# Attention and feed-forward kernel on one core: chunks 0 and 1 with reciprocals folded and transposed, trimmed scores, another split of the weight conversion, another planner

## The chip, the cores and the metric

The kernel runs on one core of a Trainium2 chip. The time is the device time of one execution in microseconds (us). The median of three runs of the kernel before is 704.7 us (704.69 to 704.81).

## What is computed

Sliding-window attention with sink columns, then a feed-forward layer with a leaky unit. There are 4 batches, 8 heads, 768 positions and a head dimension of 64; the feed-forward layer takes 512 columns to 2048 and back. Inputs are float32 but for the feed-forward weights, which are float64.

```python
scores = scale * np.matmul(q, k.transpose(0, 1, 3, 2))
keep = is_sink | in_window          # pos < 4, or 0 <= row - column < 128
scores = np.where(keep, scores, -1000000000.0)
scores = scores - np.max(scores, axis=-1, keepdims=True)
a = np.exp(scores)
a = a / (np.sum(a, axis=-1, keepdims=True) + 1e-09)
x = np.matmul(a, v)                 # heads side by side: [3072, 512]
h = x @ w_in
g = np.maximum(h, 0.0) + alpha * np.minimum(h, 0.0)
return (g @ w_out).astype(np.float32)
```

## The kernel before

The 3072 rows are cut into 12 chunks of 256 rows (c; three to a batch). A chunk's attention comes first and its feed-forward part behind it. The 2048 inner columns are cut into 16 blocks (f).

**Feed-forward.** Operands are split into a high and a low part of reduced precision, so each product is three matmuls. A first block (`gemm1`, L740, 12 matmuls of 256 columns) takes xh and xl with the weights' two parts. ScalarE then does one activation (L744), VectorE a maximum (L745), ScalarE casts the high part gh (L746), VectorE subtracts for gl (L747). The second block (`gemm2`, L777 and L778 with gh, L775 with gl, 6 matmuls of 512 columns) adds into two banks that stay open over a chunk; it runs two blocks behind its first (LAG).

**Weights.** The 16 weight blocks arrive as pairs of 32-bit words, 1 MB each, and are converted once, by f, in `convert_weights`: ScalarE takes the high words without sign and with a new exponent (L337); VectorE shifts left by three (L340), ors the sign in (L341), ors in the three bits from the low words (L343); ScalarE casts the high part (L348); VectorE subtracts for the low part (L351).

**Attention of chunks 0 and 1** (`SPLIT`). Scores are plain float32 matmuls of 260 columns on two heads at a time in row tiles (L528), then masked row minimum on VectorE (L550) and exponential on ScalarE (L554). `finish_head` transposes each head's unnormalised weights (L573, L574) and copies them out (comb, L578 on ScalarE or L579). `sink_step` makes the reciprocals of the row sums (L611, L613) and the transposed sink weights (L617, L618, L623, L625). `av` for each pair of heads then spreads the reciprocals over a bank with small matmuls against the identity (`ones`, L666), copies them to rb (L669, ScalarE), adds sinks (L670) and values (L680) in the bank's other half, multiplies by rb (L687, VectorE), and splits the product into xh (L691, ScalarE) and xl (L694, VectorE).

**Attention of chunks 2 to 11.** Scores are two reduced-precision matmuls of 260 columns (L537, L538) for each head and half (u) of the chunk. The weights are normalised by head (L583, L584, L591, L595), transposed (`trans`, L637), multiplied by a triangle mask (L641) and used in `av` (chunk 2) or `av_two` (chunks 3 on, L705, L720). In the first half of a batch's first chunk, `soften` reads the last 132 of the 260 score columns only (`w0`).

**What sets the order.** The program first records every operation with a cost, an engine and the values it reads and writes. `Plan.issue` then draws from this record: it holds a clock for each engine, takes for each the operation that can start first (ties by rank, which is the place of the TensorE operation that needs it), and writes the instructions in that order. The order of each engine is thereby fixed before the run. What is recorded in which order is the table `order` at L902 and following: LEAD = 5 blocks of chunk 0, then chunk 1's blocks in turn with chunk 0's rest, so that each weight is used by chunk 1 LEAD blocks after chunk 0; then chunks 2 to 11. `work` puts chunk 1's attention over the first LEAD blocks, chunk 2's over the LATE = 14 blocks ahead of its own, and every later one over the chunk before (SPAN = 12). `convert(f + 2)` keeps the weights two blocks ahead of their first use. `vs_prep` makes the high and low part of the sink values (L410 on ScalarE, L411 on POOL). The startup loads are listed at L425 and following, in the order of their DMAs.

## Time and profile before

| | |
|---|---|
| median of three runs | 704.7 us |
| profiled execution | 704.98 us |
| its span (first to last instruction) | 703.3 us |
| TensorE matmul busy | 686.4 us, 98% |
| VectorE busy | 496.2 us, 71% |
| ScalarE busy | 397.6 us, 57% |
| POOL busy | 33.8 us, 5% |
| granted TensorE clock, mean | 0.994 of full |
| DMA, mean over the span | 91 GB/s |

In the views, PE is TensorE's matmuls, PEld its weight loads, DVE VectorE, ACT ScalarE, POOL GpSimd. An instruction is named by its line in the kernel and by what it writes and reads, as out<-in. A bracket at a row's end is the time for which the engine stood idle before it, and whose work ended that wait. An engine's busy time is no measure of what it costs: which wait ended last is read stage by stage.

### The profile page before, as it was taken

The page shows a single profiled execution, that of the slowest core. Times are in us where ns is not written, and L with a number is a line of the kernel's source. Part 1 is how long each engine was busy: PE and PEld are TensorE (multiplying, and loading weights), DVE is VectorE, ACT ScalarE, POOL GpSimd, SP SyncE. Part 2 cuts the span into 40 slices and gives each one's busy share as a digit, 9 for nine tenths or more (in the row PEclk, how much of TensorE's full clock was granted, in tenths as well). Part 3 has the DMA queues.
Part 4 walks back from the last instruction along what each step waited for, and adds up shares of the span by engine and source line. Part 5 has one row for each costly group of instructions (what it writes and reads, how often), then busy time and mean ns, then how long its engine had stood idle before and what let it go on. Part 6 is the DMA issues. An engine that isn't in the chain of part 4 may idle for free.

```text
span 703.3 us, 13425 instructions
## 1 busy us (share of the span) xinstructions
PE 686.4 (98%) x4737; PEld 600.1 (85%) x4739; DVE 496.2 (71%) x1665; ACT 397.6 (57%) x1090; POOL 33.8 (5%) x116
## 2 busy tenths in 40 slices
PE   7999999989999999999999999999999999999996
PEld 3577898978989989989989988988988988998985
DVE  6699999987746956965964973974974884884331
ACT  5797667856626726735835734843843852753332
POOL 3000000001000000000000000000000000000000
PEclk9899999999999999999999999999999999999999
DMA  8548810443212312321412321420420321300000
GB/s 317 198 142 293 300 65 20 124 126 100 57 47 79 104 46 84 96 59 56 115 43 71 96 61 47 136 62 23 126 76 27 108 76 46 102 6 23 31 2 34
DMA packets 28156, 63.71 MB, mean 91 GB/s; under 512 B 2992, under 2 KB 9136, under 8 KB 28080
## 3 DMA queue, kind: packets, MB, share of 16 engines
q1 hardware_dynamic: 24528, 49.66, 23.3%
q10 hardware_dynamic: 3552, 13.11, 5.2%
q8 instruction: 39, 0.64, 0.4%
q14 instruction: 37, 0.30, 0.1%
HBM read 56.47 MB, written 6.29 MB: 89 GB/s over the span
## 4 chain that ended last, share of the span: by engine, by line
PE 85%; DVE 10%; ACT 2%; issue 2%; DMA 0%; POOL 0%; ACTq 0%; DVEq 0%
PE bank L740 34%; PE bank L775 11%; PE bank L777 11%; PE bank L778 11%; PE bank L720 4%; PE bank L537 3%; PE bank L538 3%; PE bank L637 2%; DVE wa L343 2%; DVE wa L341 2%; DVE w L351 1%; DVE wa L340 1%; PE bank L680 1%; DVE g L745 1%; PE bank L528 1%
## 5 line engine op out<-in xcount | busy, mean ns | idle before, releaser
L740 PE MATMUL bank<-xh,w 128*128 128x256 f32 x1536 | 309.0, 282 | 2.4 <-DVE g L745 2.4
L740 PEld LDWEIGHTS bank<-xh,w 128*128 128x128 f32 x1536 | 250.8, 188 | 9.8 <-DVE g L745 3.3
L740 PE MATMUL bank<-xl,w 128*128 128x256 f32 x768 | 214.3, 279 | 0.5 <-DVE xl L694 0.5
L744 ACT ACTIVATE g<-bank,param 128x256 f32<-128x256 f32 x192 | 89.7, 469 | 140.0 <-PE bank L740 136.4
L777 PE MATMUL bank<-w,gh 128*128 128x512 f32 x382 | 152.4, 399 | 0.0
L778 PE MATMUL bank<-w,gh 128*128 128x512 f32 x382 | 149.7, 392 | 0.0
L740 PEld LDWEIGHTS bank<-xl,w 128*128 128x128 f32 x768 | 144.6, 188 | 5.4 <-DVE xl L694 0.7
L745 DVE TENSOR_TENSOR g<-bank,g 128x256 f32<-128x256 f32 x192 | 80.5, 420 | 87.1 <-ACT g L744 86.7
L775 PE MATMUL bank<-w,gl 128*128 128x512 f32 x382 | 120.4, 397 | 0.0
L746 ACT CAST gh<-g 128x256 fp32r<-128x256 f32 x192 | 77.2, 403 | 74.2 <-DVE g L745 73.4
L554 ACT ACTIVATE pt<-pt,nm 128x260 f32<-128x260 f32 (+1 forms) x192 | 94.5, 493 | 38.5 <-DVE nm L550 35.9
L747 DVE TENSOR_TENSOR gl<-g,gh 128x256 fp32r<-128x256 f32 x192 | 80.9, 422 | 41.1 <-ACT gh L746 38.9
L550 DVE CUSTOM_DVE_ANT_0 pt<-bank,masks 128x260 f32<-128x260 f32 (+1 forms) x192 | 75.9, 400 | 16.2 <-PE bank L538 10.9
L775 PEld LDWEIGHTS bank<-w,gl 128*128 128x128 f32 x382 | 70.0, 188 | 16.2 <-issue 1.7
L777 PEld LDWEIGHTS bank<-w,gh 128*128 128x128 f32 x382 | 71.8, 188 | 8.5 <-ACT comb L578 0.3
L778 PEld LDWEIGHTS bank<-w,gh 128*128 128x128 f32 x382 | 71.8, 188 | 8.2
L641 DVE TENSOR_TENSOR wa<-bank,tri 128x512 f32<-128x512 f32 x80 | 50.6, 684 | 15.2 <-PE bank L637 15.2
L506 DVE TENSOR_TENSOR kq<-stage,kq 64x392 fp32r<-64x392 f32 x80 | 45.2, 565 | 7.6 <-ACT kq L504 5.4
L537 PE MATMUL bank<-kq 128*128 128x260 f32 x160 | 45.0, 285 | 0.5 <-DVE nm L550 0.5
L595 DVE CUSTOM_DVE_ANT_0 comb<-pt,ri 128x128 f32<-128x128 f32 x136 | 44.5, 346 | 0.7
L599 POOL TENSOR_TENSOR sink<-pt,ri 128x8 f32<-128x8 f32 x80 | 20.1, 254 | 513.9 <-DVE ri L584 213.3
L538 PE MATMUL bank<-kq 128*128 128x260 f32 x160 | 44.6, 282 | 0.0
(119 smaller groups left out, 693.5 us busy)
## 6 DMA issues: line engine op xcount, KB each, us to landing
stage<-qk SPq DMA_DIRECT2D x80, 324.0 KB, 2.8
wraw<-w ACTq DMA_DIRECT2D x12, 1024.0 KB, 5.2
v<-vp SPq DMA_DIRECT2D x44, 192.0 KB, 2.5
out_dram<-ob SPq DMA_DIRECT2D x22, 256.0 KB, 2.2
wraw<-w SPq DMA_DIRECT2D x4, 1024.0 KB, 11.1
lent<-pairs SPq DMA_DIRECT2D x4, 324.0 KB, 6.1
stage<-pairs SPq DMA_DIRECT2D x4, 324.0 KB, 6.6
ob<-vs SPq DMA_DIRECT2D x4, 256.0 KB, 3.1
```

The costliest lines, as they stand in the source:

```text
L537: nc.tensor.matmul(s[:, :WIN], qh()[:, qs], ks()[:, ko:ko + WIN], start=True, stop=False)
L538: nc.tensor.matmul(s[:, :WIN], ql()[:, qs], ks()[:, ko:ko + WIN], start=False, stop=True)
L550: op("DVE", dve(n), lambda: nc.vector.tensor_tensor_reduce(out=pt.at[:, u, w0], in0=s.at[:, w0], in1=masks[:, i, w0], scale=-0.125, scalar ...
L554: op("ACT", exp(n), lambda: nc.scalar.activation(pt.at[:, u, w0], pt.at[:, u, w0], AF.Exp, bias=nm.at[:, h, u:u + 1], scale=-1.0, accum_ou ...
L740: nc.tensor.matmul(h(), fin.at[:, 0, part, ks], rhs.at[:, kt], start=(kt == 0 and n == 0), stop=(kt == KT - 1 and n == 2))
L744: op("ACT", act(QC, True), lambda: nc.scalar.activation(g.at, h(), AF.Copy, scale=alt[:, f:f + 1]), reads=[bk, known("param")], writes=[g])
L745: op("DVE", dve(QC), lambda: nc.vector.tensor_tensor(g.at, h(), g.at, ALU.max), reads=[bk], writes=[g])
L746: op("ACT", cast(QC), lambda: nc.scalar.copy(gh.at, g.at), reads=[g], writes=[gh])
L747: op("DVE", dve(QC), lambda: nc.vector.tensor_tensor(gl.at, g.at, gh.at.bitcast(F32), ALU.subtract), reads=[g, gh], writes=[gl])
L775: nc.tensor.matmul(o2[j].at, gl.at[:, js], fin.at[:, 1, 0], start=False, stop=(f == NF - 1))
L777: nc.tensor.matmul(o2[j].at, gh.at[:, js], fin.at[:, 1, 0], start=(f == 0), stop=False)
L778: nc.tensor.matmul(o2[j].at, gh.at[:, js], fin.at[:, 1, 1], start=False, stop=False)
```

## The change

Five parts.

1. Chunks 0 and 1: `av` gives way to `av_split` on two pairs of heads. ScalarE (or VectorE) folds the reciprocals out to a 512-wide tile (L669 of the changed kernel), TensorE transposes it in four pieces into one bank (L745), ScalarE copies the bank (L748), sinks and values of both pairs go into one bank (L754, L711), and one 512-wide multiply (L762), one cast (L766) and one subtraction (L770) end it. Two rb tiles of 256 become one of 512.
2. Scores that nobody reads are left out: in the first half of each batch's first chunk, 132 columns in place of 260.
3. Weight blocks 8 to 15 (LATER): ScalarE writes the three low bits (L386), and one VectorE instruction shifts and ors (L389); the instruction L340 of before falls away for these. Blocks 0 to 7 keep their instructions, the low bits ahead of the sign.
4. The low part of batch 0's sink values is made on VectorE (L460) and no longer on POOL; the loads at the start come in another order.
5. The planner: an engine takes the operation of lowest rank among those that can start within 0.2 us (TensorE 0.1 us) of the first that can; costs of split scores and of changes of tiling are other; LEAD is 7; chunk 1's attention is recorded over the first OVER = 4 blocks.

```diff
@@
 SLACK = 0.5
+WAIT = {"DVE": 0.2, "ACT": 0.2, "PE": 0.1}
...
-LEAD = 5
+LEAD = 7
+OVER = 4
 LATE = 14
 SPAN = 12
 AHEAD = 4
+LATER = 8
...
+                    if pick and t > pick + WAIT.get(e, 0.0):
+                        continue
...
+                    found.append((t, rank[o], i, o, e, real))
+                    if pick is None or t < pick:
+                        pick = t
+                if found:
+                    w = pick + WAIT.get(e, 0.0)
+                    mine = min((x for x in found if x[0] <= w), key=lambda x: x[1:3])
+                    if best is None or mine[:2] < best[:2]:
...
-                    cost += 0.16
+                    cost += 0.16 if "col" in (o.mode, mode) else 0.1
...
-        op("DVE", dve(n, True), lambda: nc.vector.tensor_scalar(wa.at, wa.at, 3, None, op0=ALU.logical_shift_left), writes=[wa])
+        if f < LATER:
+            op("DVE", dve(n, True), lambda: nc.vector.tensor_scalar(wa.at, wa.at, 3, None, op0=ALU.logical_shift_left), writes=[wa])
+            op("DVE", dve(n), lambda: nc.vector.scalar_tensor_tensor(
+                wa.at, low(), 29, wa.at, op0=ALU.logical_shift_right, op1=ALU.bitwise_or), reads=[raw], writes=[wa])
+        else:
+            three = held(None)
+            op("ACT", act(n), lambda: nc.scalar.activation(
+                low(), raw.at.bitcast(U16).rearrange("p x (w s) -> p x w s", s=2)[:, :, 0, 1], AF.Copy, scale=2.0 ** -13, bias=-0.5 + 2.0 ** -14),
+                reads=[raw], writes=[three])
+            op("DVE", dve(n), lambda: nc.vector.scalar_tensor_tensor(
+                wa.at, wa.at, 3, low(), op0=ALU.logical_shift_left, op1=ALU.bitwise_or), reads=[raw, three], writes=[wa])
         op("DVE", dve(n), lambda: nc.vector.scalar_tensor_tensor(
         op("DVE", dve(n), lambda: nc.vector.scalar_tensor_tensor(
             wa.at, high(), -0x80000000, wa.at, op0=ALU.bitwise_and, op1=ALU.bitwise_or), reads=[raw], writes=[wa])
-        op("DVE", dve(n), lambda: nc.vector.scalar_tensor_tensor(
-            wa.at, low(), 29, wa.at, op0=ALU.logical_shift_right, op1=ALU.bitwise_or), reads=[raw], writes=[wa])
...
-        op("POOL", pool2(DM), lambda: nc.gpsimd.tensor_tensor(t.at[D:], raw.at[D:], t.at[D:].bitcast(F32), ALU.subtract), reads=[raw], writes=[t])
+        engine, on, cost = ("POOL", nc.gpsimd, pool2(DM)) if b else ("DVE", nc.vector, dve(DM))
+        op(engine, cost, lambda: on.tensor_tensor(t.at[D:], raw.at[D:], t.at[D:].bitcast(F32), ALU.subtract), reads=[raw], writes=[t])
...
+    then(lambda: load_head(0, 4))
     then(lambda: load_weights(0, "SP"))
     then(lambda: vs_prep(0))
+    then(lambda: load_head(0, 6))
     then(lambda: load_v(0, 0))
-    then(lambda: load_head(0, 4))
-    then(lambda: load_head(0, 6))
     then(lambda: load_v(0, 2))
...
+        w0 = slice(0 if c % CPB or u else P, WIN)
+        n = w0.stop - w0.start
+        kw = slice(ko + w0.start, ko + WIN)
...
-                    nc.tensor.matmul(bk.at[:, :WIN], st.at[r, :QC][:, qs], st.at[r, QC:][:, ko:ko + WIN], start=True, stop=True)
-            op("PE", native(WIN) + 0.02, scores, reads=used, writes=banks_, tail=N_TAIL)
+                    nc.tensor.matmul(bk.at[:, w0], st.at[r, :QC][:, qs], st.at[r, QC:][:, kw], start=True, stop=True)
+            op("PE", 1.47 * native(n), scores, reads=used, writes=banks_, tail=N_TAIL, mode="row")
...
-                nc.tensor.matmul(s[:, :WIN], qh()[:, qs], ks()[:, ko:ko + WIN], start=True, stop=False)
-                nc.tensor.matmul(s[:, :WIN], ql()[:, qs], ks()[:, ko:ko + WIN], start=False, stop=True)
-            op("PE", 2 * mm(WIN), scores, reads=[kq], writes=banks_, tail=R_TAIL)
+                nc.tensor.matmul(s[:, w0], qh()[:, qs], ks()[:, kw], start=True, stop=False)
+                nc.tensor.matmul(s[:, w0], ql()[:, qs], ks()[:, kw], start=False, stop=True)
+            op("PE", 2 * mm(n), scores, reads=[kq], writes=banks_, tail=R_TAIL)
...
-            r = rinv[c, g] = val("ri")
+            r, wide = val("ri"), val("ob")
+            rinv[c, g] = wide
...
+            op("DVE", 0.16, lambda: nc.vector.reciprocal(four(), four()), writes=[r])
+            each = lambda: r.at.rearrange("p (h u) -> p u h", u=2).unsqueeze(3).broadcast_to([P, 2, 4, D])
+            fold = lambda: wide.at.rearrange("p (u h d) -> p u h d", u=2, h=4)
+            op("ACT", cast(8 * D), lambda: nc.scalar.copy(fold(), each()), reads=[r], writes=[wide],
+               other=("DVE", dve(8 * D, True), lambda: nc.vector.tensor_copy(fold(), each())))
...
-            def ones():
-                for u in range(2):
-                    for j in range(2):
-                        x = 2 * (p % 2) + j
-                        nc.tensor.matmul(r()[j * D:(j + 1) * D, u * P:(u + 1) * P],
-                                         rv.at[:, 2 * x + u:2 * x + u + 1].broadcast_to([P, D]), ident, start=True, stop=True)
-            op("PE", native(P), ones, reads=[rv, known("ident")], writes=[(bk, 1)], tail=N_TAIL, mode="col")
...
+    def av_split(c, g):
+        both = (2 * g, 2 * g + 1)
+        src, v = [wt.pop((c, x)) for x in both], [vtile.pop((c, x)) for x in both]
+        wide, rb = rinv[c, g], val("rb")
+        rk = val("o" if c == 0 else "pa")
+
+        def inverse():
+            for n in range(2):
+                for u in range(2):
+                    nc.tensor.transpose(rk.at[:, (2 * n + u) * P:(2 * n + u + 1) * P],
+                                        wide.at[:, (2 * u + n) * P:(2 * u + n + 1) * P], ident)
+        op("PE", 4 * TURN, inverse, reads=[wide, known("ident")], writes=[rk], tail=T_TAIL)
+        op("ACT", cast(4 * P, True), lambda: nc.scalar.copy(rb.at, rk.at), reads=[rk], writes=[rb])
+        bk = val("pa")
+        vt, st = vst[c // CPB], sinkT[c]
+
+        def sinks():
+            for n, x in enumerate(both):
+                nc.tensor.matmul(bk.at[:, n * QC:(n + 1) * QC], vt.at[:, x * P:(x + 1) * P], st.at, start=n == 0, stop=False)
+        op("PE", 2 * mm(QC), sinks, reads=[vt, st], writes=[bk], tail=R_TAIL)
+
+        def both_values():
+            for n in range(2):
+                values(c, v[n].at, lambda j: src[n][j].at, bk.at[:, n * QC:(n + 1) * QC], n == 1)
+        op("PE", 2 * values_cost(c), both_values, reads=[t for two in src for t in two] + v, writes=[bk], tail=N_TAIL, mode="col")
+        x1, x2 = begin_x(c, 2 * g)
+        op("DVE", dve(4 * P), lambda: nc.vector.tensor_tensor(rb.at, bk.at, rb.at, ALU.mult), reads=[bk], writes=[rb])
+        view = lambda: rb.at.rearrange("p (n x) -> p n x", n=2)
+        part = slice(2 * g, 2 * g + 2)
+        keys = [(x1, x) for x in both], [(x2, x) for x in both]
+        op("ACT", cast(4 * P), lambda: nc.scalar.copy(x1.at[:, part], view()), reads=[rb], writes=keys[0])
+        if c and not g:
+            for x in both:
+                load_v(c, x + 2)
+        op("DVE", dve(4 * P), lambda: nc.vector.tensor_tensor(x2.at[:, part], view(), x1.at[:, part].bitcast(F32), ALU.subtract),
+           reads=[rb, *keys[0]], writes=keys[1])
...
-    several("rb", 2, [P, QC], F32)
+    several("rb", 1, [P, 2 * QC], F32)
...
-            for at, st in ((8, lambda: av(c, 3)), (8, lambda: av(c, 2)), (8, lambda: sk(1)),
-                           (6, lambda: av(c, 1)), (5, lambda: av(c, 0)), (4, sk)):
+            for at, st in ((8, lambda: av_split(c, 1)), (8, lambda: sk(1)), (5, lambda: av_split(c, 0)), (4, sk)):
...
-    work = spread(attention(1), LEAD)
+    work = spread(attention(1), OVER) + [[] for _ in range(LEAD - OVER)]
...
```

`values` holds the value matmuls of `av` as they were, on a bank given to it; `begin_x` opens xh and xl. `link`, `draw` and `issue` are the former `issue` in three functions.

**VectorE, second half of chunk 0's softmax beside the first weight block.** wa_85 is the first weight's working tile, ri_93 the first four heads' reciprocals, ts_100 their sink weights, pt_79 and pt_80 the masked scores of two heads. Before:

```order
L340 TENSOR_SCALAR wa_85<-wa_85 128x1024
L341 SCALAR_TENSOR_TENSOR wa_85<-wraw,wa_85 128x1024
L611 TENSOR_SCALAR ri_93<-sm_91 128x8
L343 SCALAR_TENSOR_TENSOR wa_85<-wraw,wa_85 128x1024
L617 CAST ts_100<-sink_87 128x4x32
L613 RECIPROCAL ri_93<-ri_93 128x8
L550 ISA pt_79,nm_89<-bank_64,masks 128x132
L550 ISA nm_89 128x1
L618 TENSOR_TENSOR ts_100<-sink_87,ts_100 128x4x32
L550 ISA pt_80,nm_89<-bank_65,masks 128x132
```

In the changed kernel:

```order
L381 TENSOR_SCALAR wa_85<-wa_85 128x1024
L460 TENSOR_TENSOR vs_102<-ob_103,vs_102 64x512
L664 TENSOR_SCALAR ri_93<-sm_91 128x8
L674 CAST ts_100<-sink_87 128x4x32
L675 TENSOR_TENSOR ts_100<-sink_87,ts_100 128x4x32
L666 RECIPROCAL ri_93<-ri_93 128x8
L602 ISA pt_79,nm_89<-bank_64,masks 128x132
L602 ISA nm_89 128x1
L602 ISA pt_80,nm_89<-bank_65,masks 128x132
L602 ISA nm_89 128x1
L382 SCALAR_TENSOR_TENSOR wa_85<-wraw,wa_85 128x1024
L391 SCALAR_TENSOR_TENSOR wa_85<-wraw,wa_85 128x1024
```

The low part of the sink values (L460) has come in, the sink weights and the two softmax rows (L550, now L602) stand ahead of both or instructions of the weight, and in before they stood behind both.

**TensorE, middle of chunk 2's attention.** comb_82 and comb_83 are normalised weights of two pairs of heads, sinkT_101 and vs_102 the sinks, wa_85 and v_76 weights and values, bank_65 takes chunk 3's scores; xh_106 is an input of the feed-forward block. Before:

```order
L637 MATMUL bank_67<-ident,comb_82 128x128 x4
L775 MATMUL bank_66<-w_1226,gl_115 128x512
L775 MATMUL bank_64<-w_1226,gl_115 128x512
L537 MATMUL bank_65<-kq_74 128x260
L538 MATMUL bank_65<-kq_74 128x260
L670 MATMUL bank_66<-sinkT_101,vs_102 128x256
L680 MATMUL bank_66<-wa_85,v_76 64x256 x2
L680 MATMUL bank_66<-wa_85,v_76 64x128 x4
L637 MATMUL bank_67<-ident,comb_83 128x128 x4
L537 MATMUL bank_65<-kq_75 128x260
L538 MATMUL bank_65<-kq_75 128x260
```

In the changed kernel:

```order
L806 MATMUL bank_69<-xh_106,w_1129 128x256
L725 MATMUL bank_66<-sinkT_101,vs_102 128x256
L711 MATMUL bank_66<-wa_85,v_76 64x256 x2
L711 MATMUL bank_66<-wa_85,v_76 64x128 x4
L806 MATMUL bank_69<-xh_106,w_1129 128x256
L806 MATMUL bank_69<-xl_108,w_1129 128x256
L806 MATMUL bank_69<-xh_106,w_1129 128x256 x2
L806 MATMUL bank_69<-xl_108,w_1129 128x256
L806 MATMUL bank_69<-xh_106,w_1129 128x256 x2
L806 MATMUL bank_69<-xl_108,w_1129 128x256
L806 MATMUL bank_69<-xh_106,w_1129 128x256
L843 MATMUL bank_67<-w_1046,gh_113 128x512
```

Before, sinks, values, transposes and scores follow each other with no feed-forward matmul among them; in the changed kernel sinks and values of a pair stand between the matmuls of a first block (L806 is L740 of before).

## Rows read from the trace of the kernel before

**Rows 1.** Busy time by stretch: start:end, length, then PE, PEld, DVE, ACT, POOL, clock.

```profile
28.00:52.00 24.00, 23.47 (x172) 16.08 (x171) 23.72 (x62) 21.45 (x61) 2.62 (x8) 1.00 0.47 148
52.00:73.40 21.40, 19.05 (x151) 14.80 (x150) 20.21 (x39) 16.59 (x38) 1.33 (x2) 1.00 0.85 310
73.40:100.00 26.60, 26.60 (x174) 24.16 (x173) 26.54 (x42) 18.21 (x33) 0.00 (x0) 1.00 0.58 198
73.40:182.10 108.70, 105.08 (x709) 93.32 (x708) 97.15 (x284) 72.91 (x183) 4.79 (x15) 1.00 0.35 109
182.00:703.30 521.30, 515.58 (x3600) 463.51 (x3598) 338.55 (x1217) 270.19 (x763) 19.19 (x69) 1.00 0.22 65
```

**Rows 2.** The chain that ended last, shares of the span by engine.

```profile
PE 85%; DVE 10%; ACT 2%; issue 2%; DMA 0%; POOL 0%; ACTq 0%; DVEq 0%
```

**Rows 3.** Timeline of VectorE, startup: start, duration, engine, line, operation.

```profile
11.80 2.24 DVE L341 SCALAR_TENSOR_TENSOR wa<-wraw,wa 128x1024 int32<-128x1024 int32 x1
...
21.49 0.30 DVE L550 CUSTOM_DVE_ANT_0 pt<-bank,masks 128x132 f32<-128x132 f32 x1 [2.46 <-PE bank L528]
...
23.33 0.42 DVE L687 TENSOR_TENSOR rb<-bank,rb 128x256 f32<-128x256 f32 x1 [1.54 <-ACT rb L669]
...
25.16 0.42 DVE L694 TENSOR_TENSOR xl<-rb,xh 128x256 fp32r<-128x256 f32 x1 [1.20 <-ACT xh L691]
```

**Rows 4.** Timeline of POOL, startup.

```profile
11.69 1.27 POOL L411 TENSOR_TENSOR vs<-ob,vs 64x512 fp32r<-64x512 f32 x1 [3.28 <-ACT vs L410]
```

**Rows 5.** Timeline of TensorE, startup.

```profile
15.77 1.65 PE L528 MATMUL bank<-lent 64*128 64x260 f32 x4 [2.09 <-DVE nm L550]
```

**Rows 6.** Groups by line, whole span: count, busy us, mean ns, idle before.

```profile
L341 DVE SCALAR_TENSOR_TENSOR wa<-wraw,wa 128x1024 int32<-128x1024 int32 x16 | 20.5, 1282 | 0.1
L337 ACT ACTIVATE wa<-wraw 128x1024 f32<-128x1024 f32 x16 | 18.4, 1151 | 3.9 <-DVE w L351 3.8
L340 DVE TENSOR_SCALAR wa<-wa 128x1024 int32<-128x1024 int32 x16 | 10.9, 685 | 0.5 <-ACT wa L337 0.5
L666 PE MATMUL bank<-ident,ri 128*64 128x128 f32 x64 | 5.6, 304 | 0.0
L641 DVE TENSOR_TENSOR wa<-bank,tri 128x512 f32<-128x512 f32 x80 | 50.6, 684 | 15.2 <-PE bank L637 15.2
L506 DVE TENSOR_TENSOR kq<-stage,kq 64x392 fp32r<-64x392 f32 x80 | 45.2, 565 | 7.6 <-ACT kq L504 5.4
```

**Rows 7.** Timeline of VectorE, last subtraction of chunk 1's attention.

```profile
69.41 0.42 DVE L694 TENSOR_TENSOR xl<-rb,xh 128x256 fp32r<-128x256 f32 x1
```

**Rows 8.** Timeline of TensorE, from the last wait ahead of the full stretch.

```profile
71.96 0.38 PE L740 MATMUL bank<-xh,w 128*128 128x256 f32 x1 [1.57 <-DVE g L745]
...
73.42 0.39 PE L777 MATMUL bank<-w,gh 128*128 128x512 f32 x1
...
76.19 0.39 PE L777 MATMUL bank<-w,gh 128*128 128x512 f32 x1
```

**Rows 9.** Timeline of TensorE, chunk 2's attention.

```profile
148.29 0.28 PE L538 MATMUL bank<-kq 128*128 128x260 f32 x1
148.41 0.40 PE L777 MATMUL bank<-w,gh 128*128 128x512 f32 x1
...
154.55 0.39 PE L670 MATMUL bank<-sinkT,vs 128*128 128x256 f32 x1 [1.44 <-DVE wa L641]
154.86 1.09 PE L680 MATMUL bank<-wa,v 128*64 128x256 f32 x12
155.88 0.66 PE L637 MATMUL bank<-ident,comb 128*128 128x128 f32 x4
156.30 0.36 PE L740 MATMUL bank<-xh,w 128*128 128x256 f32 x1
```

**Rows 10.** Groups by line, TensorE, 73.4 to 182.1 us.

```profile
L777 PE MATMUL bank<-w,gh 128*128 128x512 f32 x65 | 25.5, 393 | 0.0
...
L537 PE MATMUL bank<-kq 128*128 128x260 f32 x30 | 8.8, 298 | 0.5 <-DVE nm L550 0.5
```

More of the change, by code (lines that the diff above doesn't have):

```diff
@@ L1 @@
+from bisect import insort
 from collections import deque
@@ new lines, in draw @@
+            clock[e] = t + cost
+            if o.locks and (e == "DVE" or e == "POOL"):
+                lock = t + cost
+            if o.nbytes:
+                dma = max(dma, t + 1.5) + o.nbytes / 290e3
+                end = dma + 0.5
+            else:
+                end = t + cost + o.tail
+            for v in o.values:
+                left[v] -= 1
+                if not left[v] and v.kind:
+                    insort(free[v.kind], (end + self.HOP, at[v]), key=lambda f: f[0])
+            for a in o.after:
+                i = a.index
+                x = t + cost if e == a.engine == "PE" else end + self.HOP
+                ready[i] = max(ready[i], x)
+                sure[i] = max(sure[i], x + (0.0 if e == "PE" else SLACK))
+                missing[i] -= 1
+                if not missing[i]:
+                    for w in a.ways:
+                        open_[w].append(a)
@@ L675, in av @@
         sets.append((2, slice(3 * P, 4 * P), slice(P, 2 * P)))
[L677 to L682 removed]
+        for n, (blk, ws, os) in enumerate(sets):
+            for j in range(2):
+                nc.tensor.matmul(a[j * D:(j + 1) * D, os], v[:, blk, j], weights(j)[:, ws], start=False, stop=stop and n == len(sets) - 1)
```

209 lines of the change are left out of this document (94 added, 115 removed).

## The prediction

> **What bounds the kernel now.** I read the chain of waits first: TensorE holds 85% of it and VectorE 10% [rows 2]. The busy times by stretch say where each counts. From 182 us to the end TensorE is busy for 515.6 of 521.3 us [rows 1], so there only matmul time and TensorE's own waits count. From 28 to 73 us VectorE is busy for 43.9 of 45.4 us: weights, chunk 1's attention and the first blocks share it. From 73.4 to 100 us both are full (26.60 and 26.54 of 26.60), while ScalarE has 8.4 us free [rows 1]. In the timeline, TensorE's last wait of that start is the one of 1.57 us on L745; from 73.42 us it runs without a gap [rows 8] up to chunk 2's attention, where it waits 1.44 us for the mask multiply L641 [rows 9]. So three numbers are wanted: how early the state of 73.42 us is reached, what the waits around 154 us are worth, and how many matmul nanoseconds go.
>
> The profiled execution took 704.98 us, its span 703.3; the sum is made against 704.98, and the median of the runs stands 0.28 below. A measurement of this kernel can tell some 0.2% (1.4 us) from no change: faster is below 703.3, slower above 706.1.
>
> **Startup, to 28 us.** VectorE waits 2.46 us for scores (L528), 1.54 for the copy of the reciprocals (L669), 1.20 for xh (L691), and the sign instruction L341 takes 2.24 us [rows 3] where the other fifteen average 1.22 ((20.5 − 2.24)/15, [rows 6]); POOL's L411 ran beside it from 11.69 for 1.27 us [rows 4]. Together 6.2 us. The change attacks each. L411's work goes to VectorE, where a 64x512 subtraction is bounded by half and all of L641's 0.68 for 512 elements [rows 6]; I take 0.6, plus 0.45 for one comb copy that the new order gives to VectorE (near the 0.42 of a 256-wide pass, [rows 3]). The order rows show the softmax of the last heads ahead of the weight's ors; the 2.09 us that scores waited at 15.77 us for L550 [rows 5], which stood behind those ors, is what made VectorE wait 2.46 us later. The first weight's load stands behind 324 KB more, some 1.1 us at the 310 GB/s of a full stretch [rows 1]; the softmax now placed ahead covers it, and if that cover fails the first weight is 1.1 us late. All gone, it is −6.2 + 1.05 = −5.2; none gained, 0. The folded path is a serial chain of its own (fold, four transposes, copy, values, multiply, cast), so I leave 0.7 of waiting: **−4.5**.
>
> **28 to 73 us.** LEAD = 7 and OVER = 4 put more in front of chunk 1's last xl, which ends at 69.83 us now [rows 7]. Counted along both VectorE orders: one weight's two ors more (2 × 1.22), one block's maximum and subtraction more (2 × 0.42), one head's preparation less (0.57 [rows 6] and 0.43), six multiplies and subtractions of 256 (0.42 each, [rows 3]) against three of 512 (0.68, by L641, the nearest row) −0.5: +1.8, less small ones, +1.6. ScalarE gets 3.2 us more (an L337 of 1.15 [rows 6], a low-bit pass, folds, an activation), against 7.4 us that it has free there [rows 1]; a quarter of it taken as exposed, +0.8 (ends 0 and 3.2). So the last xl ends at 69.8 − 4.5 + 1.6 + 0.8 = 67.7. By then TensorE has done half a first block less and one second block more than at 73.42 us; both halves of a pair count 2.77/2 us (76.19 − 73.42, [rows 8]), so it is 0.7 ahead: 67.0. Behind that xl, weight 7 still needs 2.6 us of VectorE while TensorE has 1.6 us of work: +1.0. For waits on L745 like the 1.57 one I allow another 1.0. 69.0 against 73.42: **−4.4**. The removed `ones` (64 matmuls, 5.6 us busy, two at a time [rows 6]) give way to 16 transposes of 0.105 us (four from 155.88 to 156.30, [rows 9]); half lie in the start, where TensorE waits anyhow, so I count nothing, with −1.2 as the far end.
>
> **73 to 145 us.** VectorE's conversion for f ≥ 8 loses one L340 each, 8 × 0.685 = 5.5 us [rows 6], and ScalarE gains eight low-bit passes. TensorE has no gap here now [rows 1], so a lighter VectorE yields nothing; but LEAD = 7 needs each weight two blocks, 5.5 us, earlier, and the 5.5 us pays for just that. The low-bit pass on ScalarE shows in no row; the nearest is L337, 1.15 us with 1024 elements at the same 8-byte distance. A pair of pairs (5.54 us) leaves ScalarE 8.39/26.6 × 5.54 = 1.75 us free, so 1.15 fits: **0**. Its far end is L341's disturbed 2.24 us: 8 × 0.49 = +3.9.
>
> [...]
>
> **Chunk 2's attention.** From 73.4 to 182.1 us are 108.7 us, 105.1 busy [rows 1]: 3.6 us of plain waiting. By count: L777 runs twice in a second block, and 64 such (the 65th opens the next) are 32 pairs [rows 10], × 2.77 = 88.6; 60 score matmuls (30 and 30) of 0.12 us (148.41 − 148.29) = 7.2; four sets of values of 1.02 (155.88 − 154.86), four of transposes of 0.42, four of sinks of 0.31 = 7.0 [rows 9]. That is 102.8, so up to 5.9 us are lost. The order rows show sinks and values of a pair between feed-forward matmuls in the changed kernel, where before they followed each other and L641. Ends: −5.9 and 0 (or worse, if the waits only move). I take **−3.8**, near the plain waits.
>
> **Trimmed scores.** Chunks 3, 6 and 9: 3 × 8 × 2 = 48 matmuls from 260 to 132 columns, now 0.12 us. By columns 0.061 (−2.8 us); no gain, 0; at the pace of plain float32, 640 columns in the 1.02 us of a value set, 1.6 ns each, 0.21 us (+4.3). The nearest row in size is the transposes' 0.105 for 128 columns: 48 × 0.015 = **−0.6**. Chunk 0's trimmed scores lie in the start and are in its term.
>
> **Steady state.** The TensorE order from about 182 us is all but the same: 0.
>
> Sum: −4.4 − 3.8 − 0.6 = −8.8; 696.2 for a profiled execution, **696.0** as median.
>
> **Rivals.**
> - *The start's gain is lost* (17%): the fold chain replaces the waits by its own, or the weights, needed 5.5 us earlier, come late and TensorE waits for L351 in the leading blocks. For: VectorE is full to 100 us. Against: the 5.5 us taken off it. 696.2 + 4.4 − 0.3 = 700.3.
> - *The hole stays or moves* (10%): L641 and the normalisation are late again. For: VectorE still does it all. 699.7.
> - *Trimmed scores run at the float32 pace* (7%): no row has a reduced-precision matmul under 256 columns. 696.0 + 0.6 + 4.3 = 700.9.
> - *The change does not do what it says* (5%): start and hole both as before. 704.2, within 0.2%.
> - *Slower* (6%): ScalarE becomes the bound of 73 to 122 us. Its low-bit pass reads two bytes in eight, a form that no row has. Each us above the free 1.75 delays eight weights, and behind them the blocks that need them; 8 × (d − 1.75) exceeds 8.8 from d = 2.85 us. At d = 3.5 it is +14.0, so 710. Against: L337's 1.15 at the same distance.
>
> **Numbers.** The forecast has 55%. Its own range is 696.0 with −0.7 (startup), −2.1 (hole), −2.2 (scores) and the allowance of 1.0 as the low end, 690.5 rounded; the four rivals on the high side up to 701 lie inside 702.0. Left out are the last two (11%) and what lies beyond the far ends. Faster 0.55 + 0.17 + 0.10 + 0.07 = 0.89; same 0.05; slower 0.06.
>
> **What would show it.** Right: VectorE's waits of 2.46, 1.54 and 1.20 us gone before 28 us; the first sign instruction at 1.22; chunk 1's last subtraction (L770) ending near 67.7; TensorE without gaps from about 69; waits of at most 2.1 us about chunk 2's attention; trimmed L537-like matmuls 0.105 us apart; the low-bit pass at 1.05 to 1.2 us. Wrong: TensorE waits on L351 or on xl after 70 us, a low-bit pass over 1.75 us, trimmed scores over 0.12 us, or a new wait in the steady stretch.

## The result and the profile after

The changed kernel takes 695.81 us as median of four runs (695.09 to 696.52); the kernel before took 704.70 (704.11 to 704.81) beside it. The ratio is 0.9875 with a 95% interval of 0.9858 to 0.9893, so it is faster by 8.9 us. The profiled execution took 695.24 us, its span 693.3, 10.0 us less than before's. Busy time by stretch in the changed kernel (length, then PE, PEld, DVE, ACT, POOL, granted clock):

```profile
10.00:28.00 18.00, 16.95 (x112) 9.72 (x116) 16.25 (x46) 17.05 (x48) 2.73 (x6) 1.00 0.84 311
28.00:52.00 24.00, 21.48 (x142) 15.90 (x143) 23.35 (x52) 21.91 (x55) 3.16 (x6) 0.93 0.71 249
52.00:69.00 17.00, 16.33 (x116) 13.84 (x115) 16.48 (x30) 15.68 (x33) 0.87 (x2) 1.00 0.49 182
69.00:100.00 31.00, 30.39 (x199) 27.47 (x200) 30.84 (x48) 27.91 (x47) 0.00 (x0) 1.00 0.55 191
100.00:145.00 45.00, 44.89 (x299) 39.96 (x299) 40.98 (x145) 29.54 (x83) 1.62 (x8) 1.00 0.27 82
145.00:166.00 21.00, 20.33 (x150) 17.50 (x151) 14.51 (x53) 13.12 (x39) 2.04 (x4) 1.00 0.32 102
166.00:182.00 16.00, 16.00 (x111) 14.73 (x110) 14.44 (x61) 11.56 (x36) 1.04 (x5) 1.00 0.28 85
182.00:693.30 511.30, 505.51 (x3541) 455.22 (x3539) 335.00 (x1189) 267.53 (x747) 17.85 (x66) 1.00 0.21 65
```

From 69 to 182 us TensorE stands idle for 113.0 − (30.39 + 44.89 + 20.33 + 16.00) = 1.4 us, where before it stood for 3.6 in 73.4 to 182.1 [rows 1]. ScalarE is now nearly as full as VectorE up to 100 us. The clock, which was at 0.83 or less from 15 to 24 us before (first fence), now falls later, from 38 to 42 us (second):

```profile
15.00:18.00 3.00, 1.89 (x5) 1.20 (x7) 2.09 (x13) 1.44 (x3) 0.00 (x0) 0.53 1.02 400
18.00:21.00 3.00, 3.00 (x16) 1.69 (x14) 1.03 (x1) 1.73 (x7) 0.19 (x1) 0.50 1.04 411
21.00:24.00 3.00, 3.00 (x27) 1.82 (x23) 0.94 (x5) 1.10 (x6) 0.19 (x1) 0.83 0.62 229
```

```profile
36.00:39.00 3.00, 1.97 (x10) 1.40 (x10) 2.84 (x11) 2.62 (x7) 0.96 (x2) 0.86 0.79 318
39.00:42.00 3.00, 3.00 (x16) 2.34 (x15) 2.97 (x8) 2.75 (x10) 0.17 (x1) 0.58 0.37 107
```

VectorE's timeline in the changed kernel, for [rows 3, 7]: the three waits are gone, the first sign and or instructions take their 1.22 us, and chunk 1's last subtraction ends at 66.4 us.

```profile
14.49 1.22 DVE L382 SCALAR_TENSOR_TENSOR wa<-wraw,wa 128x1024 int32<-128x1024 int32 x1
15.75 1.23 DVE L391 SCALAR_TENSOR_TENSOR wa<-wraw,wa 128x1024 int32<-128x1024 int32 x1
...
19.29 0.29 DVE L602 CUSTOM_DVE_ANT_0 pt<-bank,masks 128x132 f32<-128x132 f32 x1
...
19.71 0.69 DVE L762 TENSOR_TENSOR rb<-bank,rb 128x512 f32<-128x512 f32 x1
...
22.08 0.68 DVE L770 TENSOR_TENSOR xl<-rb,xh 128x512 fp32r<-128x512 f32 x1
...
65.73 0.68 DVE L770 TENSOR_TENSOR xl<-rb,xh 128x512 fp32r<-128x512 f32 x1
```

**Where the time went.** The order of first blocks differs, but their number at a point of the work does not, so each trace is read at three points: the start of the 17th first block (193rd matmul of L740, now L806), of the 49th (577th), and of the 189th. Before, these are at 96.9, 211.8 and 683.4 us. Between the first two lies chunk 2's attention, between the last two the stretch that repeats. Offsets against before in us, profiled executions, with the medians of the runs:

| kernel | 17th | 49th | 189th | median us |
|---|---|---|---|---|
| changed | −5.9 | −8.8 | −10.1 | 695.8 |
| e1 all columns | −4.7 | −7.6 | −8.5 | 696.9 |
| e2 no window | −6.4 | −6.6 | −7.0 | 697.5 |
| e3 small matmuls | −0.3 | −3.4 | −4.7 | 700.5 |
| e4 low bits on VectorE | −4.9 | −0.6 | −1.9 | 702.7 |
| e5 sinks on POOL | −4.6 | −5.3 | −6.6 | 699.7 |
| e6 LEAD 5 | −4.3 | −5.4 | −6.7 | 698.7 |
| e7 clock held | −5.3 | −8.6 | −9.9 | 695.0 |
| e8 before, clock held | −1.9 | −1.9 | −1.9 | 704.1 |
| e9 before, folded | +4.4 | +2.7 | +2.5 | 707.3 |
| e10 small matmuls, clock held | −2.4 | −5.3 | −6.6 | 698.6 |
| e11 old loads | −5.3 | −6.0 | −7.3 | 698.1 |
| e12 two more on ScalarE | −4.2 | −3.8 | −5.1 | 698.7 |

The medians stand beside runs of the kernel before on the same chip, whose medians were 704.74 (e1 to e4), 704.74 (e5 to e8) and 704.26 (e9 to e12). A row of offsets is one execution. Those of e2 and e12 are the longest of their four runs: 698.36 us against 697.11 to 697.57, and 700.19 against 698.49 to 698.93.

### The profile page after: what moved, and what is told of

Its sections match the earlier page's. It is cut to its first block, busy times and chain, and to the rows that moved or that the text cites. A ratio compares the mean times of both kernels' runs of the same rounds, so it can differ in the third digit from the quotient of the medians.

```text
span 693.3 us, 13330 instructions
## 1 busy us (share of the span) xinstructions
PE 680.6 (98%) x4694; PEld 598.1 (86%) x4696; DVE 497.2 (72%) x1651; ACT 408.2 (59%) x1093; POOL 32.2 (5%) x115
## 4 chain that ended last, share of the span: by engine, by line
PE 86%; DVE 9%; ACT 3%; issue 1%; POOL 0%; DMA 0%; ACTq 0%; DVEq 0%
PE bank L806 35%; PE bank L841 12%; PE bank L843 12%; PE bank L844 11%; PE bank L711 5%; PE bank L589 3%; PE bank L590 3%; PE bank L694 3%; DVE wa L391 2%; DVE w L399 1%; ACT pt L606 1%; DVE wa L389 1%; ACT wa L377 1%; DVE gl L813 1%; DVE g L811 1%
## 5 line engine op out<-in xcount | busy, mean ns | idle before, releaser
L806 PE MATMUL bank<-xh,w 128*128 128x256 f32 x1536 | 314.2, 283 | 1.4 <-DVE g L811 1.2
L806 PEld LDWEIGHTS bank<-xh,w 128*128 128x128 f32 x1536 | 252.7, 189 | 9.2 <-DVE g L811 2.0
L806 PE MATMUL bank<-xl,w 128*128 128x256 f32 x768 | 214.6, 279 | 0.0
L844 PE MATMUL bank<-w,gh 128*128 128x512 f32 x382 | 149.9, 392 | 0.0
L806 PEld LDWEIGHTS bank<-xl,w 128*128 128x128 f32 x768 | 145.1, 189 | 5.2
L811 DVE TENSOR_TENSOR g<-bank,g 128x256 f32<-128x256 f32 x192 | 80.4, 420 | 88.6 <-ACT g L810 87.8
L606 ACT ACTIVATE pt<-pt,nm 128x260 f32<-128x260 f32 (+1 forms) x192 | 94.2, 491 | 24.5 <-DVE nm L602 23.9
L602 DVE CUSTOM_DVE_ANT_0 pt<-bank,masks 128x260 f32<-128x260 f32 (+1 forms) x192 | 75.0, 402 | 15.2 <-PE bank L590 11.9
L844 PEld LDWEIGHTS bank<-w,gh 128*128 128x128 f32 x382 | 71.9, 188 | 8.3
L555 DVE TENSOR_TENSOR kq<-stage,kq 64x392 fp32r<-64x392 f32 x80 | 45.2, 566 | 10.1 <-ACT kq L553 8.1
L553 ACT CAST kq<-stage 128x392 fp32r<-128x392 f32 x80 | 41.5, 519 | 8.9 <-PE bank L590 6.2
L590 PE MATMUL bank<-kq 128*128 128x260 f32 (+1 forms) x160 | 44.3, 281 | 0.0
L589 PE MATMUL bank<-kq 128*128 128x260 f32 (+1 forms) x160 | 43.8, 278 | 0.1
```

Of the source, the lines that this page charges most:

```text
L589: nc.tensor.matmul(s[:, w0], qh()[:, qs], ks()[:, kw], start=True, stop=False)
L590: nc.tensor.matmul(s[:, w0], ql()[:, qs], ks()[:, kw], start=False, stop=True)
L602: op("DVE", dve(n), lambda: nc.vector.tensor_tensor_reduce(out=pt.at[:, u, w0], in0=s.at[:, w0], in1=masks[:, i, w0], scale=-0.125, scalar ...
L606: op("ACT", exp(n), lambda: nc.scalar.activation(pt.at[:, u, w0], pt.at[:, u, w0], AF.Exp, bias=nm.at[:, h, u:u + 1], scale=-1.0, accum_ou ...
L806: nc.tensor.matmul(h(), fin.at[:, 0, part, ks], rhs.at[:, kt], start=(kt == 0 and n == 0), stop=(kt == KT - 1 and n == 2))
L811: op("DVE", dve(QC), lambda: nc.vector.tensor_tensor(g.at, h(), g.at, ALU.max), reads=[bk], writes=[g])
```

## The experiments

**e1, trimming undone.** The matmuls of L580, L589 and L590 take all 260 columns; every engine's order stays.

```diff
...
-                nc.tensor.matmul(s[:, w0], qh()[:, qs], ks()[:, kw], start=True, stop=False)
+                nc.tensor.matmul(s[:, :WIN], qh()[:, qs], ks()[:, ko:ko + WIN], start=True, stop=False)
...
```

> The changed kernel with all 260 score columns again (chunks 0, 3, 6, 9, first half); every engine's order stays. My theory: in the trace of the changed kernel the two trimmed matmuls of a head start 60 and 113 ns apart where untrimmed ones take 119 each, so 24 heads times 65 ns = 1.6 us come back in chunks 3, 6 and 9, and the sixteen float32 matmuls of chunk 0 add up to 1 us in the startup: 697.0 to 698.5 as median. Rival (the forecast's price, 15 ns each): 0.7 us, 696.5. Rival (trimming mattered in the start only): no difference behind 200 us.

696.91 us, ratio to before 0.9899 (0.9877 to 0.9922), 1.1 over the changed kernel, but not where I said. The two intervals overlap (the changed kernel's is 0.9858 to 0.9893), so the pieces are read from the traces. The offset to the changed kernel is 1.2 at the 17th block, 1.2 at the 49th and 1.6 at the 189th: chunk 0's trimmed float32 matmuls are worth some 1.2 us in the start, chunk 3 nothing that can be read, and chunks 6 and 9 some 0.2 us each. Why so little is seen in TensorE's timeline of one head, in the changed kernel and in this one:

```profile
317.00 0.22 PE L589 MATMUL bank<-kq 128*128 128x132 f32 x1
317.06 0.28 PE L590 MATMUL bank<-kq 128*128 128x132 f32 x1
317.17 0.44 PE L843 MATMUL bank<-w,gh 128*128 128x512 f32 x1
317.45 0.40 PE L844 MATMUL bank<-w,gh 128*128 128x512 f32 x1
```

```profile
318.19 0.28 PE L589 MATMUL bank<-kq 128*128 128x260 f32 x1
318.31 0.28 PE L590 MATMUL bank<-kq 128*128 128x260 f32 x1
318.43 0.40 PE L843 MATMUL bank<-w,gh 128*128 128x512 f32 x1
318.66 0.39 PE L844 MATMUL bank<-w,gh 128*128 128x512 f32 x1
```

From the first score matmul to L844 it is 0.45 us trimmed and 0.47 untrimmed: the first of the pair gains 60 ns, and the long matmul behind holds its successor back by 50 (0.28 against 0.23). My expectation took the first gap for the gain; the forecast's 15 ns a matmul was close.

**e2, the planner's window off.** Rank decides only between operations that can start at the same time, as before; costs, LEAD and all else as changed.

```diff
-WAIT = {"DVE": 0.2, "ACT": 0.2, "PE": 0.1}
+WAIT = {}
```

> The changed kernel with the planner's window set to nothing, so that each engine again takes the operation that can start first. My theory: the gaps about chunk 2's attention were closed by the order in which its sinks and values are drawn, so they come back (2.4 to 3.5 us between 140 and 175 us), and the start loses part of its gain: 699 to 701. Rival: LEAD and the lighter VectorE closed them, then the gaps stay closed and the time is within 1 us of 695.8.

697.50 us, 0.9898 (0.9881 to 0.9914). The start did not lose (−6.4 against −5.9). The stretch of chunk 2's attention gains 0.2 us here where the changed kernel gains 2.9, but not because the gaps came back. Between the 17th and the 49th block TensorE stands idle for 3.6 us in the kernel before, 0.8 in the changed kernel and 1.3 here, and the wait of 1.44 us for the mask multiply [rows 9] is missing here too. Of the 2.6 us that this execution takes more than the changed kernel there, 0.5 are idle time and 2.1 longer busy time; the clock is at half from 157 to 161 us:

```profile
157.16 0.40 PE L806 MATMUL bank<-xh,w 128*128 128x256 f32 x1 [0.62 <-DVE g L811]
```

```profile
156.00:159.00 3.00, 2.36 (x12) 2.14 (x12) 2.94 (x13) 2.72 (x11) 0.00 (x0) 0.73 0.48 139
159.00:162.00 3.00, 3.00 (x15) 2.63 (x14) 1.96 (x9) 1.99 (x6) 0.36 (x2) 0.70 0.28 93
```

The three other runs are some 1 us shorter at a mean clock of 0.995 to 0.996 and not 0.993, so they probably lack that fall; they have no trace. So my theory fails for the gaps: they stay mostly closed without the window. The rival is not shown either, since runs below with LEAD = 7 and the window stand idle for 2.8 us in this stretch (e5, e11). From the 49th to the 189th block e2 gains 0.4 where the changed kernel gains 1.3: the window is worth 0.9 us in the stretch that I had called unchanged.

**e3, small matmuls put back.** `av_split` gives way to the former work on one pair, without the fold.

```diff
...
-            for at, st in ((8, lambda: av_split(c, 1)), (8, lambda: sk(1)), (5, lambda: av_split(c, 0)), (4, sk)):
+            for at, st in ((8, lambda: av_ones(c, 3)), (8, lambda: av_ones(c, 2)), (8, lambda: sk(1)),
+                           (6, lambda: av_ones(c, 1)), (5, lambda: av_ones(c, 0)), (4, sk)):
```

> The changed kernel with chunk 0's and 1's values done as before: one pair at a time, reciprocals spread by small matmuls against the identity, multiplies and subtractions 256 wide. My theory: VectorE has six more narrow passes and TensorE eight more rounds of small matmuls in the start, together 1.5 to 3 us at the point where TensorE becomes full, nothing behind it: 697.3 to 698.8. Rival (the folded chain was the cure of the startup waits): all of the 5.9 us of the start come back, 701.7. Rival (that part is hidden): 695.8 within 0.5.

700.53 us, 0.9950 (0.9934 to 0.9966): 4.7 us over the changed kernel, and all of it in the start (−0.3 at the 17th block), beyond my range and near the rival's. Its clock is low for longer (36 to 48 us: 0.95, 0.50, 0.50, 0.91), which e10 takes apart.

**e10, the same with the clock held.** As e3, with the unread matmuls of e7.

> The changed kernel with the small matmuls and narrow passes put back (as in the third run) and with the unread matmuls that keep TensorE busy between 28 and 45 us (as in the seventh). Theory A: most of the 4.7 us lost in the third run is the half clock that its trace shows from 38 to 46 us; held, 2 us or more come back: at most 698.5. Theory B: it is VectorE's narrow passes and the waits on them, and the clock is worth what it was in the seventh run, 0.8 us: 699.4 to 700.2.

698.57 us, 0.9920 (0.9903 to 0.9937), with the clock at 1.00 from 36 to 48 us. 2.0 us come back, between the two theories' numbers at their border: of e3's 4.7 us about 2 are the low clock that its waits bring on, and against e7 (the clock held in both) 3.6 us remain for the narrow passes, the small matmuls and the order that the planner draws with them. (The two ran on different chips, where the kernel before takes 704.74 and 704.26 us.)

**e9, the fold alone in the kernel before.** `av_split`, the fold and the single 512-wide rb, nothing else of the change (its diff is the one of the change for these functions).

> The kernel before with the first part of the change alone: reciprocals folded, transposed and copied 512 wide, values of two pairs in one bank, 512-wide multiply, cast and subtraction; planner, LEAD, loads, weights and score columns as before. My theory (from the run with the small matmuls put back): this part is the larger half of the start's gain, 3 to 5 us; the gaps about chunk 2's attention stay: 699.7 to 701.7. Rival: it gains only in the new planner's order, and here the time is within 1 us of 704.7.

707.27 us, 1.0041 (1.0028 to 1.0053): **slower** by 3.0 us, so a part that is missed by 3.6 us or more when the changed kernel goes without it costs 3 us when the old one takes it in. The timelines of VectorE, ScalarE and TensorE from 67 us show how:

```profile
67.07 1.22 DVE L351 TENSOR_TENSOR w<-wa,w 128x1024 fp32r<-128x1024 f32 x1
68.21 0.69 DVE L740 TENSOR_TENSOR rb<-bank,rb 128x512 f32<-128x512 f32 x1
```

```profile
68.33 1.14 ACT L337 ACTIVATE wa<-wraw 128x1024 f32<-128x1024 f32 x1 [1.34 <-DVE w L351]
69.37 0.20 ACT L337 ACTIVATION_READ_ACCUMULATOR wa<-wraw 128x1 f32 x1
69.47 0.61 ACT L744 CAST xh<-rb 128x512 fp32r<-128x512 f32 x1
```

```profile
70.13 0.38 PE L794 MATMUL bank<-xh,w 128*128 128x256 f32 x1 [3.03 <-ACT xh L744]
...
71.29 0.39 PE L794 MATMUL bank<-xl,w 128*128 128x256 f32 x1 [0.78 <-DVE xl L748]
...
73.89 0.58 PE L794 MATMUL bank<-xh,w 128*128 128x256 f32 x1 [1.75 <-DVE g L799]
```

The wide multiply stands behind weights that were ready a little earlier, the cast of xh behind another weight's first pass; TensorE waits 3.03, 0.78 and 1.75 us for what it needs next, and its clock is at 0.56 and 0.50 in the two stretches from 72 to 78 us. Between the 17th and the 49th block this kernel gains 1.7 us (table), with the old planner and the old LEAD: there, too, a redrawn order moves the time. This is the rival of the prediction in which the folded chain replaces the old waits by its own, and the planner decides whether it comes.

**e4, the low bits on VectorE for all weights.**

```diff
-LATER = 8
+LATER = 16
```

> The changed kernel with all sixteen weights converted as blocks 0 to 7 are, so no low-bit pass on ScalarE. My theory: VectorE is full from 28 to 100 us and has 5.5 us more to do by the last conversion, while LEAD = 7 wants each weight two blocks earlier; TensorE waits for the weights' low part: 2 to 5 us, 698 to 701. Rival: VectorE's work behind 73 us has room (TensorE is the only bound there), 695.8 within 0.5. [...]

702.74 us, 0.9974 (0.9961 to 0.9987): 6.9 us over the changed kernel, more than expected. Only 1.0 of it is in the start. Most of the rest comes at 126 us, and not by a late weight: scores wait for VectorE's L602, which is behind. VectorE's last conversion (L399) starts at 112.5 us here and at 106.5 in the changed kernel.

```profile
126.78 0.39 PE L589 MATMUL bank<-kq 128*128 128x260 f32 x1 [0.42 <-DVE nm L602]
...
127.91 0.36 PE L589 MATMUL bank<-kq 128*128 128x260 f32 x1 [0.62 <-DVE nm L602]
...
129.49 0.39 PE L589 MATMUL bank<-kq 128*128 128x260 f32 x1 [1.11 <-DVE nm L602]
...
130.61 0.56 PE L589 MATMUL bank<-kq 128*128 128x260 f32 x1 [0.62 <-ACT kq L553]
```

```profile
126.00:129.00 3.00, 1.34 (x6) 0.59 (x4) 2.84 (x13) 2.96 (x11) 0.20 (x1) 1.00 0.59 173
129.00:132.00 3.00, 1.89 (x8) 1.72 (x9) 2.85 (x13) 2.55 (x8) 0.20 (x1) 0.65 0.74 192
132.00:135.00 3.00, 3.00 (x14) 2.84 (x13) 1.35 (x8) 1.63 (x5) 0.21 (x1) 0.50 0.78 258
135.00:138.00 3.00, 3.00 (x16) 2.63 (x15) 1.73 (x10) 1.70 (x6) 0.21 (x1) 0.71 0.01 3
```

These waits sum to 2.8 us, and TensorE works on at half clock for nearly 7 us. From the 17th to the 49th block e4 takes 7.2 us more than the changed kernel: 3.5 more of idle TensorE (4.3 against 0.8) and 3.6 more of busy time, near the 3.4 us by which the clocks of the three stretches from 129 us (0.65, 0.50, 0.71) fall short of full, an estimate from the fence. So in this order the low-bit passes on ScalarE are worth most of the change's margin, about half of it by the clock; the planner's order was redrawn with them. A pass over 1024 elements took 0.685 us on VectorE (L340, [rows 6]) and 1.17 on ScalarE (L386 in the changed kernel), a ratio of 1.7, and VectorE was the fuller engine: in e4 it is busy for 2.96 to 3.00 of every 3 us from 96 to 111 us, ScalarE for 1.04 to 2.61. The 1.17 is near the 1.15 taken from L337 [rows 6].

**e12, two more low-bit passes on ScalarE** (LATER = 6, with the clock held as in e7).

> The seventh run's kernel (the clock held) with the low bits of weights 6 and 7 on ScalarE too. My theory: ScalarE is busy for 15.7 of 17 us from 52 to 69 us and 27.9 of 31 from 69 to 100, so two more passes of about 1.2 us find no free time and TensorE waits for gh and for the weights' high part: 0.5 to 2.5 us over 695.0. Rival: VectorE is the tighter of the two there, and 1.4 us less on it gives 0.3 to 1 us: 694.0 to 694.7.

698.74 us, 0.9918 (0.9902 to 0.9935), 3.7 over e7: slower as expected, by more. But in its trace TensorE's longest waits from 60 us on are on L606 (the line that is L602 in the changed kernel: 0.92 us at 74.8, 1.43 at 157.2), and for gh once 0.19. VectorE in turn waits for ScalarE between 28 and 130 us: 1.2 us for the activation (L814) and 0.8 for the low-bit pass (L390), waits that e7 lacks. So ScalarE has a part in it, but its share against that of the new order is not shown. In the profiled execution, the longest of the four, the clock also falls, from 159 to 163 us.

**e5, e6, e11: one other part undone each.** The sinks' low part on POOL; LEAD at 5; the startup loads in their old order.

```diff
-        engine, on, cost = ("POOL", nc.gpsimd, pool2(DM)) if b else ("DVE", nc.vector, dve(DM))
+        engine, on, cost = "POOL", nc.gpsimd, pool2(DM)
```

> The changed kernel with the low part of batch 0's sink values on POOL again, as for the other batches. My theory: POOL's subtraction and VectorE's weight instruction beside it slow each other as before (1.0 us on L341 there), against 0.69 us that VectorE no longer does itself; the start is 0.3 to 1.0 us later: 696.1 to 696.9. Rival (the move was a main part of the start's gain): 2 us or more, over 697.8. Rival (no contention in the new order): 695.1 to 695.5.

```diff
-LEAD = 7
+LEAD = 5
```

> The changed kernel with LEAD at 5 as before (chunk 1's attention still over 4 blocks). My theory: five leading blocks give TensorE less to do while chunk 1's softmax and the weights share VectorE, so it waits for chunk 1's xl and its clock may fall again: 1 to 4 us, 696.8 to 699.8. Rival: the later use of each weight makes up for it, and the time is within 0.5 us of 695.8. The gaps about chunk 2's attention stay closed by both.

```diff
-    then(lambda: load_head(0, 4))
     then(lambda: load_weights(0, "SP"))
     then(lambda: vs_prep(0))
-    then(lambda: load_head(0, 6))
     then(lambda: load_v(0, 0))
+    then(lambda: load_head(0, 4))
+    then(lambda: load_head(0, 6))
     then(lambda: load_v(0, 2))
```

> The changed kernel with the loads at the start in their old order (the first weight ahead of the third and fourth pair of heads). My theory: the first weight comes 1 us earlier and the third pair's scores later; VectorE waits for those scores as before, and the start is 0.5 to 1.5 us later: 696.3 to 697.3. Rival: no difference, 695.8 within 0.4. Rival: earlier weights gain, 694.8 to 695.3.

699.68 (0.9931, 0.9911 to 0.9952), 698.72 (0.9927, 0.9900 to 0.9954) and 698.08 us (0.9908, 0.9892 to 0.9925). In e5 the longer VectorE instruction that I expected is there: the one beside POOL's subtraction takes 2.25 us. It is L382 here, where it was L341 before, and the sign instruction L391 now takes its 1.22. That POOL is slowed in turn is not shown: its subtraction takes 1.27 us here, as in the changed kernel at 152 to 468 us, behind the last conversion (L460, 1.269 to 1.277):

```profile
12.39 1.27 POOL L460 TENSOR_TENSOR vs<-ob,vs 64x512 fp32r<-64x512 f32 x1 [3.67 <-ACT vs L458]
```

```profile
12.50 2.25 DVE L382 SCALAR_TENSOR_TENSOR wa<-wraw,wa 128x1024 int32<-128x1024 int32 x1
```

In e6 the expected wait is there, 2.09 us on L811 at 66.05 us, and the clock falls at its end (0.51 from 66 to 69 us). My prices for e5 and e11 were too low by 2.8 us and by 0.8, and e5's median lies where its rival had it (the move a main part of the start's gain), though the trace does not put it in the start. e5's runs lie in two pairs, 698.7 us at a mean clock of 0.998 and 700.6 to 700.9 at 0.993, and the median stands between them. At the 17th block e5 and e11 stand only 1.3 and 0.6 us behind the changed kernel; the rest is lost about chunk 2's attention, where all three, and e12, show the same wait, which the changed kernel lacks (row of e5, whose matmuls behind it take 0.28 and 0.40 us as ahead of it, at a mean clock of 0.998 for the execution):

```profile
157.27 0.39 PE L589 MATMUL bank<-kq 128*128 128x260 f32 x1 [1.44 <-DVE nm L602]
```

An edit in the first 20 us thus moves the planner's order 130 us later: TensorE's order in the traces of e5 and e11 differs from the changed kernel's there, and is the same again behind the 49th block. Those 2 us belong to the redrawn order and not to POOL or to a load.

**e7, the clock held.** Matmuls of 248 unread columns where the planner sees TensorE idle between 28 and 45 us.

```diff
...
+    def spare():
+        nc.tensor.matmul(banks[5][:, 264:512], idle[:, :1].broadcast_to([P, P]), idle[:, 1:].broadcast_to([P, 248]), start=False, stop=True, skip_group_check=True)
-    plan.issue(steps, fill, WARM)
+    plan.issue(steps, fill, WARM, spare, 45.0)
```

> The changed kernel with 26 matmuls more whose results nobody reads (248 columns each, in the unread half of a bank) where the planner sees TensorE idle between 28 and 45 us. My theory: TensorE's idle 33 to 38 us is what lets its clock fall to half from 38.5 to 41.7 us; held busy, it keeps the full clock, and the 1.6 us of work that the half clock costs come back in part: 694.0 to 695.3, the clock at 1.00 in all stretches. Rival (VectorE bounds this stretch, so the low clock costs nothing): 695.8 within 0.4, at a clock of 1.00. Rival (the idle matmuls stand in front of scores and delay them): 696.5 or more.

694.99 us (694.16 to 695.35), 0.9855 (0.9839 to 0.9872). The clock is at 1.00 from 36 to 45 us. The median is 0.8 us under the changed kernel's, within the expected numbers, but the intervals overlap and its profiled execution is not ahead: VectorE is busy for 8.52 of the 9 us from 36 us on, and the gain is not settled. Its median is the lowest of the study.

**e8, the kernel before with its clock held** by eight unread matmuls of 512 columns ahead of the scores that waited 2.09 us [rows 5].

```diff
...
             def scores():
+                if (c, h, u) == HOLD:
+                    for _ in range(8):
+                        nc.tensor.matmul(banks[5], idle[:, :1].broadcast_to([P, P]), idle[:, 1:].broadcast_to([P, 512]), start=True, stop=True)
```

> The kernel before with eight unread matmuls (512 columns) in the 2.09 us for which TensorE waits at 15.77 us; nothing else is changed. My theory: that wait lets the clock fall to half from 15.8 to 22.5 us, the scores take 1.65 and 1.24 us in place of 0.71, and VectorE's waits of 2.46, 1.54 and 1.20 us hang partly on it; held, 1.5 to 3 us come back: 701.7 to 703.2. Rival (those waits come from the order and the reciprocal chain alone): within 0.5 of 704.7.

704.11 us, 0.9990 (0.9981 to 1.0000): 0.6 us, nearly the rival's no difference; its profiled execution gains 1.9, with the clock at 1.00 from 12 to 24 us. VectorE's waits, for those of [rows 3], read:

```profile
19.85 0.30 DVE L554 CUSTOM_DVE_ANT_0 pt<-bank,masks 128x132 f32<-128x132 f32 x1 [0.62 <-PE bank L532]
...
21.45 0.42 DVE L691 TENSOR_TENSOR rb<-bank,rb 128x256 f32<-128x256 f32 x1 [1.29 <-ACT rb L673]
...
23.28 0.42 DVE L698 TENSOR_TENSOR xl<-rb,xh 128x256 fp32r<-128x256 f32 x1 [1.20 <-ACT xh L695]
```

The wait for scores falls from 2.46 to 0.62 us, the waits of the reciprocal chain stay at 1.29 and 1.20.

## Why the prediction was right, and where its steps were not

The forecast of 696.0 against 695.81 held, and its three terms kept their signs and their order of size. That it came within 0.2 us is luck: errors of 0.2 to 1.5 us in the terms meet, and the kernel's own runs spread by 1.4 us.

- **The start, −4.4 forecast.** −5.9 at the 17th block. The mechanism held: waits of 2.46, 1.54 and 1.20 us gone, L341's 2.24 now 1.22. The last xl of chunk 1 ended at 66.4 and not 67.7 us, and the wait for weight 7 was 0.20 us and not 1.0; the waits on the maximum (L811) up to the 17th block came to 0.5 us against the 1.0 allowed. POOL beside L341 was rightly named: in e5 the instruction that stands beside POOL's takes 2.25 us. One reason was wrong: I laid the 2.46 us to the order in which scores and weights stand. e8, with that order kept, takes it to 0.62, so most of it was TensorE's half clock (0.53 and 0.50 from 15 to 21 us, held at 1.00 in e8) behind its own wait at 15.77 us. Another piece was not priced by itself: chunk 0's trimmed scores, about 1.2 us (e1).
- **Nothing for the removed `ones`.** Held in so far as TensorE's time did not bound there; but what replaces them is worth 3.6 us with the clock held (e7 against e10, each in its own drawn order), and in the old order it costs 3.0 (e9). The forecast's working had no place for such a product of two parts.
- **73 to 145 us, 0.** Between the 17th block and chunk 2's middle nothing was gained, as forecast. That the lighter VectorE pays for LEAD = 7 fits the outcome (e4 loses 6.9 without it), by waits for softmax rows and a fallen clock, not by late weights.
- **Chunk 2's attention, −3.8.** −2.9 from the 17th to the 49th block, with nothing from chunk 3's trimmed scores (e1). The place was right, and the size 0.9 too large. The reason held in part: the wait of 1.44 us on L641 is gone in the changed kernel and in every run made from it, e2 among them. But in four of those runs (e5, e6, e11, e12) another of 1.4 us, on L602, stands in its place, which is the rival of the hole that moves. Neither the window (e2) nor LEAD decides that, and what does, beyond the order as drawn, stays open; that the changed kernel's order has no such wait was luck as far as the prediction goes.
- **Trimmed scores, −0.6.** Chunks 3, 6 and 9 give about 0.4 by e1 (1.6 at the end less 1.2 ahead of them). The pace that I chose, by rows of 128 columns, was near as a mean only: it is 60 ns for the first and a late successor.
- **Steady, 0.** Wrong by 0.9, which the window brings (e2). No wait stands there: from the 49th to the 189th block TensorE is busy without a gap in both traces, for 471.6 and 470.3 us. The gain lies at one place of each chunk, the two transposes of the sink weights (`ts`). From the start of the matmul in front of them to the start of the transposes behind them it is 0.55 us before and 0.34 in the changed kernel in the chunk shown, and 0.52 in e2; over seven chunks the mean gain there is 0.14. Why is open.

```profile
244.64 0.28 PE L740 MATMUL bank<-xh,w 128*128 128x256 f32 x1
244.91 0.44 PE L623 MATMUL bank<-ident,ts 128*128 128x128 f32 x2
245.19 0.60 PE L637 MATMUL bank<-ident,comb 128*128 128x128 f32 x4
```

```profile
235.58 0.28 PE L806 MATMUL bank<-xh,w 128*128 128x256 f32 x1
235.70 0.38 PE L680 MATMUL bank<-ident,ts 128*128 128x128 f32 x2
235.92 0.60 PE L694 MATMUL bank<-ident,comb 128*128 128x128 f32 x4
```

The prediction's sums have small slips: 48 × 0.015 is 0.72 and not 0.6, and 704.7 less 8.8 is 695.9 and not 696.0, so its own terms give 695.8. The low end adds up to 690.0 and not 690.5. The float32 pace of its third rival counts 640 columns for a value set, where the order rows have 512 for each of two heads.

In the profiled execution the sum is −10.1 and not −8.8; the medians differ by 8.9, as the runs of the changed kernel spread from 695.1 to 696.5 us. The runs' mean clocks go with it (0.995 in the two shorter, 0.994 in the two longer), but only one of them has a trace, so that the fallen clock makes that spread is likely and not shown. Of the rivals, the float32 pace did not come (60 and 110 ns), nor did the lost start, the moved hole and the slower ScalarE in the changed kernel; e9, e5 and e12 show that these three lie near. What a planner's redrawn order is worth by itself stays open: every run but e1, e7 and e8 changes it along with its edit.
